# Fifteen small, unread loads on ScalarE's queue between two copies of a decode kernel's prologue

## The chip, the cores and the metric

The kernel runs on one core of a Trainium2 chip. It is compared by device time in microseconds (us): the time from the start to the end of one launch on that core. The core has five engines that run side by side and wait for one another through semaphores: TensorE (PE in the profile, with its weight loads as PEld), VectorE (DVE), ScalarE (ACT), GpSimd (POOL) and SyncE (SP), which computes nothing here and only issues transfers. Transfers run on the core's 16 DMA engines. Both SP and ACT issue transfers in this kernel, each into a queue of its own (in the profile, queue q1 holds those of SP and q10 those of ACT).

## The reference, cut to what matters

One token for each of two sequences goes through attention over a long cache (A) and a small mixer MLP (B), and a gate mixes the two results.

```python
B, Sq, D = 2, 1, 1024
Hq, Hkv, Sk, Dh = 32, 4, 32768, 128
# A: q = x @ wq; scores of 8 query heads per kv head against a cache of 32768 keys
scores = einsum("bhqd,bhkd->bhqk", q, k) * Dh ** -0.5
a = (softmax(scores) @ v) ... @ wo
# B: with one token, the shifted mixing gives zero, so that x1 = x
b = x + gelu(layernorm(x) @ w3) @ w4          # w3: 1024 x 3584
g = sigmoid((x * gate_w).sum(-1))
return g * a + (1 - g) * b
```

All is float32. As the kernel loads them, the two caches, wq, w3, w4 and wo are some 331 MB, nearly all of what is moved.

## The kernel before

**Buffers.** Two large buffers, `ring[0]` and `ring[1]` (`flat` is the same memory seen flat), take turns: each holds one load of up to 128 rows of 64 KB (8 MB; a load of w3 has rows of 56 KB). All large loads are issued by SP, in one fixed order: two of wq, two of w3, then a pair kt and vt (keys and values) for each of the first eight half pairs, two of w4, eight more pairs kt and vt, and three of wo with four small ones into `tail`. `load` (line 222) lets SP wait until the buffer is free and then issues. Each load of `ring[0]` counts up `landed[0]`, each of `ring[1]` counts up `landed[1]`.

**Prologue.** `project` multiplies x by wq as its two parts land (line 361). When both are done, DVE copies half of the product out of PSUM (line 410) and ACT the other half (line 412, `a_q`); q is turned round by small matmuls (line 424) and laid out in `q_pad`. `project` then does the same for the normalised x and w3. Behind that DVE copies one half of the product (line 447, `d_h`) and ACT the other (line 449, `a_h`). DVE waits for both, spreads them (line 454), PE turns them round (28 small matmuls, line 462), and DVE and ACT apply the gelu (lines 466 to 478).

**Loop.** `turn` runs 16 times, once for half of a pair of batch and kv head. PE multiplies the keys (line 495, tile `sc`), DVE takes the maximum in two steps (line 574), ACT the exponentials (line 556), PE transposes them (line 508), and PE multiplies the values (line 517, tile `pv`). Two events of a turn free the buffers. DVE counts up `k_free` ahead of its second maximum (line 573), and SP then issues the next kt into `ring[0]`. The last matmul with the values is marked, and SP then issues the next vt into `ring[1]`. After eight turns `weigh` multiplies by w4, after the other eight by most of wo; a short tail ends the kernel.

**What sets the order.** Every engine runs its list in program order, and a wait holds up all that stands behind it on that engine. PE's list in the prologue is: product with wq, line 424, product with w3, line 462, first turn. DVE's list has lines 447, 454 and 466 to 478 ahead of the loop. ACT's list has line 412, line 449, line 471 and then its loop. SP's third and fourth loads behind wq (the first kt and the first vt) wait only for the two parts of the product with w3; the second kt waits for the `k_free` of the first turn.

## Time and profile before

| | us |
|---|---|
| median of 2 runs | 773.12 (773.07 to 773.16) |
| the profiled execution's own time | 773.08 |
| span of its trace, first to last instruction | 771.5 |
| PE busy (matmuls) | 472.2 (61% of the span) |
| DVE busy | 124.2 (16%) |
| ACT busy | 72.1 (9%) |
| mean granted TensorE clock | 0.772 of full speed |

The profiled execution is 0.04 us below the median, so its rows can stand for the runs. Times in the trace count from the start of the span. In a row of the timeline the first number is the start, the second the duration from the first to the last of the instructions merged into the row; what stands in brackets is how long the engine had been idle and what ended that. A row of the transfers gives the tile, the issuing queue and the time from issue to landing.

### The profile page before, as it was taken

To read this page: it belongs to the slowest core of one execution; us is meant where nothing else is said; L and a number is where in the kernel's file an instruction comes from. 1 tells how busy PE (TensorE), PEld (TensorE's weight loads), DVE (VectorE), ACT (ScalarE), POOL (GpSimd) and SP (SyncE) were. 2 spreads that over 40 slices of the span, in tenths; PEclk is the share of its full clock that TensorE was granted. 3 is DMA by queue.
4 is the path that set the end of the run, shared out by engine and by line. 5 is a ranking of instruction groups with operands and counts; after the bars stand their busy time and mean duration, and the time that the engine had idled before them with its cause. 6 is when DMAs were issued, how large, how long until landed. Compare 5 with 4: busy or idle time off the path is not lost. (4 is left out here: it accounts for less than half of the span.)

```text
span 771.5 us, 7731 instructions
## 1 busy us (share of the span) xinstructions
PE 472.2 (61%) x3316; PEld 243.6 (32%) x3316; DVE 124.2 (16%) x383; ACT 72.1 (9%) x153; POOL 4.4 (1%) x13
## 2 busy tenths in 40 slices
PE   0566765756465756465665364657564657564668
PEld 0233432434232433242331132324342324342323
DVE  1110130212020212120210020202020202020220
ACT  0000020102020102020100020202020202020200
POOL 2000000000000000000000000000000000000000
PEclk9967677677877677877676687777687777687779
DMA  9999999999999999999999999999999999999997
GB/s 381 435 436 436 435 436 436 435 435 432 435 432 435 432 432 435 435 435 435 430 428 443 432 435 435 435 432 435 435 435 435 425 435 435 432 435 425 441 419 329
DMA packets 6646, 331.46 MB, mean 430 GB/s; under 512 B 872, under 2 KB 1008, under 8 KB 1264
## 3 DMA queue, kind: packets, MB, share of 16 engines
q1 hardware_dynamic: 6496, 331.36, 99.4%
q8 instruction: 5, 0.08, 0.0%
q10 hardware_dynamic: 144, 0.01, 0.0%
q14 instruction: 1, 0.01, 0.0%
HBM read 331.36 MB, written 0.01 MB: 429 GB/s over the span
## 5 line engine op out<-in xcount | busy, mean ns | idle before, releaser
L495 PE MATMUL sc<-load,q_cur 128*32 128x512 f32 x1024 | 146.2, 727 | 116.0 <-PEq L53 116.0
L517 PE MATMUL pv<-load,pt 128*32 128x512 f32 x1024 | 125.2, 644 | 18.8 <-PEq L53 18.8
L495 PEld LDWEIGHTS sc<-load,q_cur 128*32 128x32 f32 x1024 | 65.4, 130 | 184.5 <-issue 179.4
L508 PE MATMUL sc<-wide,p 128*128 128x128 f32 x256 | 56.4, 413 | 45.6 <-PEq L53 45.6
L556 ACT ACT_TABLE_LOAD x16 | 20.5, 1283 | 529.3 <-ACTq L53 529.3
L517 PEld LDWEIGHTS pv<-load,pt 128*32 128x32 f32 x1024 | 38.8, 117 | 95.6 <-issue 95.6
L508 PEld LDWEIGHTS sc<-wide,p 128*128 128x128 f32 x256 | 51.9, 225 | 46.6 <-issue 46.6
L574 DVE TENSOR_REDUCE mx<-sc 128x1 f32<-128x512 f32 x32 | 22.1, 692 | 273.6 <-PE sc L495 273.6
L525 PE MATMUL tr<-sel,pv_sb 128*128 128x8 f32 x256 | 37.3, 282 | 23.6 <-PEq L53 23.6
L376 PE MATMUL acc<-load,w_pad 128*32 128x512 f32 x224 | 32.0, 714 | 21.0 <-PEq L53 21.0
L525 PEld LDWEIGHTS tr<-sel,pv_sb 128*128 128x128 f32 x256 | 36.3, 226 | 24.5 <-issue 24.5
L596 DVE COPY pv_sb<-pv 128x512 f32<-128x512 f32 x32 | 20.6, 686 | 137.2 <-PE tr L521 137.2
L591 DVE COPY pt<-sc 64x256 f32<-64x256 f32 x64 | 26.7, 417 | 28.6 <-PE sc L508 28.6
L561 ACT COPY pt<-sc 64x256 f32<-64x256 f32 x64 | 23.5, 368 | 36.2 <-PE sc L508 36.2
L361 PE MATMUL sc<-load,x_pad 128*32 128x512 f32 x128 | 19.6, 779 | 6.5 <-PEq L53 6.5
L376 PEld LDWEIGHTS acc<-load,w_pad 128*32 128x32 f32 x224 | 9.1, 129 | 42.3 <-issue 42.3
L556 ACT ACTIVATE p<-sc,bias 128x512 f32<-128x512 f32 x32 | 21.7, 683 | 0.2
L361 PE MATMUL sc<-load,xn_pad 128*32 128x384 f32 (+1 forms) x128 | 15.6, 648 | 6.2 <-PEq L53 6.2
L499 PE MATMUL tr<-wide,m 128*1 128x128 f32 x16 | 4.3, 269 | 18.8 <-PEq L53 18.8
L588 DVE COPY p<-p 128x256 f32<-128x256 f32 x32 | 9.4, 294 | 38.0 <-ACT p L556 38.0
L346 PE MATMUL tr<-xg_sb,perm 128*128 128x16 f32 x4 | 1.0, 372 | 23.3 <-DMA xg_sb<-xg 23.3
L501 PE MATMUL tr<-ones,mb 1*128 1x1 f32 x32 | 5.9, 253 | 11.4 <-PEq L53 11.4
(101 smaller groups left out, 141.8 us busy)
## 6 DMA issues: line engine op xcount, KB each, us to landing
load<-w SPq DMA_DIRECT2D x4, 7168.0 KB, 25.4
load<-wo SPq DMA_DIRECT2D x1, 7168.0 KB, 27.5
load<-wo SPq DMA_DIRECT2D x1, 4608.0 KB, 18.6
load<-wo SPq DMA_DIRECT2D x1, 2560.0 KB, 24.3
tail<-wo SPq DMA_DIRECT2D x1, 1024.0 KB, 26.3
tail<-wo SPq DMA_DIRECT2D x1, 640.0 KB, 27.4
load<-kt SPq DMA_DIRECT2D x16, 29.3
load<-vt SPq DMA_DIRECT2D x16, 30.9
```

What stands on the lines that cost most here:

```text
L361: last = nc.tensor.matmul(b[C * g:C * g + C, :hi - lo], pad[:, k], t[:, o + lo:o + hi], start=(k == 0), stop=(k == KD - 1))
L376: inst = nc.tensor.matmul(acc[lo:lo + C], lhsT, rows[:, g * (D // 2):(g + 1) * (D // 2)], start=False, stop=last, skip_group_check=True)
L495: last = nc.tensor.matmul(sc[i][C * g:C * g + C], q_cur[:, w, s], ring[0][:, w, o:o + 512], start=(s == 0 and w == 0), stop=(s == 1 and w ...
L508: last = nc.tensor.transpose(sc[k][:, t * P:(t + 1) * P], pair.rearrange("p w q -> p (w q)"), ident)
L517: last = nc.tensor.matmul(pv[C * g:C * g + C], pt[:, w, lo:lo + C], ring[1][:, w, o:o + G * DH], start=(w == 0 and t == 0), stop=(w == PAR ...
L525: last = nc.tensor.matmul(tr[1][:, w * REP:(w + 1) * REP], pv_sb[:, s, w].rearrange("p i q -> p (i q)"), sel[:, s], start=(s == 0), stop=( ...
L556: nc.scalar.activation(p[:, i, :, :PART], sc[i].rearrange("p (t q w) -> p t w q", t=NT, w=PART), AF.Exp, bias=bias, scale=scale, accum_out ...
L561: nc.scalar.copy(*halves(1, c)).then_inc(pt_in, 1)
L574: last = nc.vector.reduce_max(out=mx[:, i:i + 1], in_=sc[i], axis=AX.X)
L588: nc.vector.tensor_copy(p[:, i, :, PART], p[:, i, :, 0]).then_inc(to_pe, 1)
L591: nc.vector.tensor_copy(*halves(0, c)).then_inc(pt_in, 1)
L596: last = nc.vector.tensor_copy(pv_sb[:, :, :, i], pv.rearrange("p (s q w) -> p s w q", q=HALF, w=PART))
```

## The change

Directly behind its copy of wq's product (line 412), ACT waits for that copy and then issues fifteen loads into a new tile `told_sb` of 16 partitions. Load number n, from 1 to 15, has n rows, each of 16 + n floats (68 to 124 bytes), taken from the corner of the first keys. Each adds 16 to a new semaphore `told` when it has landed, and ACT's next instruction waits for all fifteen. Nothing reads `told_sb`. No other instruction, buffer or wait is changed.

```diff
+    told_sb = new("told_sb", 15, 32, parts=16)
...
+    told = sem("told")
...
     act.after(done)
     a_q = act.mark(nc.scalar.copy(row[:, 1], sc[1]))
+    act.after(a_q)
+    for n in range(1, 16):
+        nc.scalar.dma_start(told_sb[:n, n - 1, :16 + n], kt[0, 0, :n, :16 + n]).then_inc(told, 16)
+    act.after((told, 15 * 16))
```

On ACT, in the prologue, the list before reads as follows; L412 is the copy of wq's product, L449 that of w3's product, and L556 is in the loop.

```order
L336 ACT_TABLE_LOAD
L336 ACTIVATE gate<-tr 128x2
L412 COPY pt<-sc 128x512 [waits pe]
L449 COPY pt<-sc 128x384 [waits pe]
L471 ACTIVATE u<-u 128x112 [waits dve]
L553 UNCONDITIONAL_BRANCH
L556 ACT_TABLE_LOAD [waits b_in]
```

The two copies stood next to each other; their line numbers in the changed kernel are 414 and 455. On ACT with the change, the first of the new loads stand like this behind the first copy.

```order
L338 ACT_TABLE_LOAD
L338 ACTIVATE gate<-tr 128x2
L414 COPY pt<-sc 128x512 [waits pe]
L417 DMA told_sb<-kt 1x17 [waits act]
L417 DMA told_sb<-kt 2x18
L417 DMA told_sb<-kt 3x19
```

The first load waits for the copy ahead of it, and the others follow without a wait. The end of the same stretch of ACT's list, up to the gelu (L477), is this.

```order
L417 DMA told_sb<-kt 13x29
L417 DMA told_sb<-kt 14x30
L417 DMA told_sb<-kt 15x31
L455 COPY pt<-sc 128x384 [waits pe,told]
L477 ACTIVATE u<-u 128x112 [waits dve]
L559 UNCONDITIONAL_BRANCH
L562 ACT_TABLE_LOAD [waits b_in]
```

The copy of w3's product now waits for `told` beside PE; no other row of ACT has moved. The lists of PE, DVE, POOL and SP are what they were, but for line numbers.

## The prediction

> **What bounds the kernel now.** I read the page first: the span, the slices of DMA and the queues.

> ```profile
> span 771.5 us, 7731 instructions
> DMA  9999999999999999999999999999999999999997
> q1 hardware_dynamic: 6496, 331.36, 99.4%
> q10 hardware_dynamic: 144, 0.01, 0.0%
> ```

> SP's queue q1 keeps the 16 DMA engines busy for 99.4% of the span. The kernel is bound by its loads. What comes late on an engine costs time only if q1 runs empty by it; then the gap is lost for good, as no slack follows in which to win it back.

> Second I read SP's own waits, to see which events release its loads.

> ```profile
> SPq L222 <- DVEq L573: 323.1, 16, 20.7
> SPq L222 <- PE pv L517: 285.1, 16, 19.5
> ```

> Each kt is released by DVE's line 573, each vt by the values' last matmul. Third I read SP's timeline in the stretch behind the change, and the transfers by window, where a row ends with the time from issue to landing (in this order the two parts of w3, the first kt and vt, the second kt).

> ```profile
> 36.07 16.84 SPq L222 DMA_DIRECT2D load<-w  x2
> ...
> 52.58 0.33 SPq L222 DMA_DIRECT2D load<-w  x1
> 71.26 0.33 SPq L222 DMA_DIRECT2D load<-kt  x1
> 86.26 0.33 SPq L222 DMA_DIRECT2D load<-vt  x1
> 105.38 0.33 SPq L222 DMA_DIRECT2D load<-kt  x1
> 125.25 0.33 SPq L222 DMA_DIRECT2D load<-vt  x1
> ...
> load<-w SPq DMA_DIRECT2D x1, 7168.0 KB, 24.3
> ...
> load<-w SPq DMA_DIRECT2D x1, 7168.0 KB, 24.7
> ...
> load<-kt SPq DMA_DIRECT2D x1, 25.4
> load<-vt SPq DMA_DIRECT2D x1, 29.7
> ...
> load<-kt SPq DMA_DIRECT2D x1, 29.9
> ```

> The first row merges the two issues of w3: the first part is issued at its start, 36.07, and lands at 36.07 + 24.3 = 60.4, the second at 52.58 + 24.7 = 77.3, the first kt at 71.26 + 25.4 = 96.7, the first vt at 86.26 + 29.7 = 116.0, the second kt at 105.38 + 29.9 = 135.3. The spacings are 16.9, 19.4, 19.3 and 19.3: the loads stream without a gap. A load has 8 rows for each engine (128 over 16), so a 64 KB row takes 19.35 / 8 = 2.42 us, a row of w3 2.11 us.

> **How a small load from ACT fares beside that stream.** The trace has one: xg, 128 rows of 96 bytes, issued together with the first load of wq. The rows are from the window of the two issues, and from the window 4 to 23.2 us.

> ```profile
> xg_sb<-xg ACTq DMA_DIRECT2D x1, 12.0 KB, 22.5
> load<-wq SPq DMA_DIRECT2D x1, 22.3
> ...
> q1 hardware_dynamic: 144, 8.39, 100.9%
> q10 hardware_dynamic: 144, 0.01, 0.5%
> ```

> ```profile
> q1 hardware_dynamic: 1, 0.00, 11.2%
> ...
> q10 hardware_dynamic: 1, 0.00, 9.4%
> ...
> q1 hardware_dynamic: 1, 0.07, 2158.9%
> ```

> The semaphore's write of wq's load goes first, then xg's, then the next 64 KB row (0.07 MB). They alternate here too, so I count each such write as a turn.

> [...]

> **How the new loads spread.** What counts is the engine that gets most. No load of fewer than 128 rows stands in the trace, but a store does: the result, 8 rows, seen in the window 770 to 771.5.

> ```profile
> q1 hardware_dynamic: 16, 0.01, 2.1%
> out<-out_sb SPq DMA_DIRECT2D x1, 8.0 KB
> ```

> 16 packets: 8 rows and 8 writes of the semaphore, thus 8 engines with a row each. So load n uses n engines, one row and one write on each. If they always begin at the same engine, that engine serves all fifteen: 30 packets, 30 turns. If they were spread evenly, each engine would have 2 x 120 / 16 = 15. I take 30, since nothing in the row of the store speaks of a rotation; the other is a rival. [...]

> **The cost, step by step.** ACT's part of the prologue, and the issue of four small loads on SP's queue:

> ```profile
> 52.59 0.59 ACT L412 COPY pt<-sc 128x512 f32<-128x512 f32 x1 [24.11 <-PE sc L361]
> 86.27 0.48 ACT L449 COPY pt<-sc 128x384 f32<-128x384 f32 x1 [33.09 <-PE sc L361]
> 740.49 1.86 SPq L222 DMA_DIRECT2D tail<-wo  x4
> ```

> 1. Issuing: 15 x 1.86 / 4 = 7.0 us on ACT, from 53.2 to 60.2. ACT then idles until 86.27, so this costs nothing.
> 2. The turns. The first new packet is there about a microsecond after 53.2. From then to its end the first part of w3 has some 2 rows and its semaphore's write left on each engine, which is 3 turns; the second part gives 9 (8 rows, 1 write), kt 9, vt 9: 30 in all. The thirtieth lies at the end of the first vt, at 116.0 or up to 1.5 us sooner on an engine that runs ahead. It cannot lie much later, either: SP has nothing behind that vt until the second kt is released, and an engine with an empty q1 takes ACT's packets one after the other (0.5% of the engines' time for 144 of them, or 0.5% x 16 x 19.2 / 144 = 0.01 us each). With half a microsecond for the last write to be seen, the wait ends at T = 114.5 to 116.5. I take 115.3.
> 3. What the wait holds up. Line 449 starts at T in place of 86.27. Line 454 on DVE, line 462 on PE and then the first turn stand behind it, while PE has nothing else in its list.

> ```profile
> 87.00 2.08 DVE L454 COPY p<-pt 128x896 f32<-128x896 f32 x2
> 89.13 5.85 PE L462 MATMUL tr<-wide,p 128*128 128x8 f32 x28 [2.92 <-DVE p L454]
> 96.75 8.52 PE L495 MATMUL sc<-load,q_cur 128*32 128x512 f32 x64 [1.77 <-PEq L53]
> 105.44 0.69 DVE L574 TENSOR_REDUCE mx<-sc 128x1 f32<-128x512 f32 x1 [2.85 <-PE sc L495]
> ```

> From the copy to the matmuls of line 462: 89.13 - 86.27 = 2.9; these 5.85; then the keys at once, as the first kt has long landed (before, PE waited 1.77 for it); from their start to the release of the second kt 105.38 - 96.75 = 8.6. Together 17.3: the second kt is issued at T + 17.3 = 132.6, not at 105.38. DVE's gelu (lines 466 to 478) fits beside the keys, as before.
> 4. The gap. A load into an empty queue lands 22.3 after its issue (wq's row), so the second kt lands at 132.6 + 22.3 = 154.9, not at 135.3: 19.6 later. With the ends of T it is 18.8 to 20.8.
> 5. What is late next: the second vt. Before, it was issued 19.9 behind the second kt, and 1.1 of that was the wait for the first vt, which landed at 116.0 while the copies ahead were done at 115.0 (row below). So it is issued 18.8 behind, at 151.4, and could land at 173.7 from an empty queue; in the stream it lands at 154.9 + 19.35 = 174.3. No second gap, by 0.6 us. From there on all waits are as before, 19.6 later.

> ```profile
> 114.57 0.42 DVE L591 COPY pt<-sc 64x256 f32<-64x256 f32 x1 [0.44 <-PE sc L508]
> 116.12 9.07 PE L517 MATMUL pv<-load,pt 128*32 128x512 f32 x64 [1.59 <-PEq L53]
> ```

> 6. The 240 new packets themselves: 0.01 us each, 30 of them on one engine, 0.3 us; inside the ends of T. The one more semaphore and the unread tile cost nothing that a row shows.

> The sum is 19.6 us on the profiled execution's 773.08, which is 792.7; the median of the runs is 773.12, so the same. For the bounds: the nearest rows for 30 turns are xg's 9 turns in 22.5 us. From below, the wait is free as long as the second kt is still issued by 135.3 - 22.3 = 113.0, thus T up to 95.7; this is turn 20. A gain is excluded, since the change takes no byte and no wait away. From above the gap ends with q1 empty.

> **The rivals.**
> - *Spread evenly* (the loads rotate over the engines): 15 turns, 12 by 77.3 and 3 more of 2.42, so T is about 85, ahead of 86.27. Then line 449 doesn't move, and the time is 773.1. It decides from turn 20 downwards. For it speaks that the engines of a short transfer can't be named from the trace; against it nothing does but the plainness of a fixed start. The same 773.1 follows if several packets of one queue go in a turn; xg's row speaks against that.
> - *In between*: some packets pass without a full turn, and the wait ends between turn 21 and 27. Each turn saved takes 2.42 from the loss; at turn 27, T is near 109 and the time 786.
> - *Later than the empty queue*: all rows of a load on one engine. Then it has 120 + 15 packets, 105 of which are left when q1 is empty; at 0.01 us each that is 1 us, at 0.05 each 5 us: 794 to 798. The store's 8 writes speak against it.
> - *The change doesn't do what it says*, because ACT's wait isn't on the way to anything: excluded by step 3, since DVE's line 454 waits for both copies.

> **How the numbers follow.** The forecast 0.77; spread evenly, or several packets in a turn, 0.12; in between 0.07; later 0.04. The forecast's own range is 790.5 to 795.5 (the ends of T, and a microsecond each way for the chain's 17.3). The range of 0.8 takes in most of the forecast, the upper end of the in-between (784 to 788) and the lower of the later: 784 to 797. 2%, about what a measurement of this kernel can tell from no change, is 15.5 us, so the bound lies at 788.6: slower 0.81, within 2% 0.18 (the 0.12 and most of the in-between), faster 0.01.

> **What would show it.** In the profile after: q10 with 144 + 240 = 384 packets; ACT's copy of w3's product at 114.5 to 116.5, ahead of it a wait for `told` and not for PE; the first matmuls with the keys directly behind line 462's; SP's issue of the second kt near 132.6; the slices of DMA with a hole of nearly one slice (19.3 us) near 116 to 135; all later issues of SP 19 to 20 us behind those of before. It is wrong if that copy stays at 86.3 (then the turns are 15 or fewer), if it comes between 96 and 110, or if a second gap opens behind the second kt.

## The result and the profile after

The changed kernel takes 793.54 us (2 runs, 793.35 to 793.72) against 773.12 before: slower by 2.64% (ratio 1.0264, 95% interval 1.022 to 1.0308). The profiled execution's own time is 793.72, its span 792.2 us, 20.7 longer than before.

The page after, its span, its slices of DMA and its two queues:

```profile
span 792.2 us, 7747 instructions
DMA  9999972999999999999999999999999999999997
q1 hardware_dynamic: 6496, 331.36, 96.9%
q10 hardware_dynamic: 384, 0.03, 0.0%
```

SP's queue moves the same packets, but there is a hole in the sixth and seventh slice, and its share falls from 99.4% to 96.9%. ACT's queue has 240 packets more. The timeline of ACT around the hole shows where it begins:

```profile
50.87 0.58 ACT L414 COPY pt<-sc 128x512 f32<-128x512 f32 x1 [22.79 <-PE sc L363]
51.49 5.56 ACTq L417 DMA_DIRECT2D told_sb<-kt  x15
114.66 0.48 ACT L455 COPY pt<-sc 128x384 f32<-128x384 f32 x1 [63.21 <-DMA told_sb<-kt]
```

The fifteen loads are issued in 5.56 us, and the copy of w3's product, at 86.27 before, starts at 114.66. What ends its wait is no longer PE's product, but the small loads. The waits of the stretch 50 to 140 us (engine and line, what it waited for, total, times, longest) show who was held up by it:

```profile
ACT pt L455 <- DMA told_sb<-kt: 63.2, 1, 63.2
...
PE tr L468 <- DVE p L460: 31.0, 1, 31.0
DVE p L460 <- ACT pt L455: 28.1, 1, 28.1
```

DVE waits 28.1 us for ACT's copy, and PE behind it 31.0. The timeline of DVE, PE and SP, taken engine by engine, carries this on to the loads:

```profile
115.24 2.08 DVE L460 COPY p<-pt 128x896 f32<-128x896 f32 x2 [28.11 <-ACT pt L455]
...
117.38 6.14 PE L468 MATMUL tr<-wide,p 128*128 128x8 f32 x28 [31.00 <-DVE p L460]
123.45 8.99 PE L501 MATMUL sc<-load,q_cur 128*32 128x512 f32 x64
...
86.44 0.33 SPq L224 DMA_DIRECT2D load<-vt  x1
132.57 0.33 SPq L224 DMA_DIRECT2D load<-kt  x1
149.31 0.33 SPq L224 DMA_DIRECT2D load<-vt  x1
```

The second kt is issued at 132.57 in place of 105.38. The windows 117 to 132, 132 to 134 and 149 to 150 us of the transfers show the queue empty and then full again:

```profile
DMA packets 1, 0.02 MB, mean 1 GB/s; under 512 B 0, under 2 KB 0, under 8 KB 0
...
q8 instruction: 1, 0.02, 0.4%
...
load<-kt SPq DMA_DIRECT2D x1, 22.9
...
load<-vt SPq DMA_DIRECT2D x1, 25.5
```

In 15 us a single packet moves, a piece of the program (queue q8). The second kt lands at 132.57 + 22.9 = 155.5 (before 135.3, so 20.2 later), the second vt at 149.31 + 25.5 = 174.8, again 19.3 behind it: no second gap opens between the two.

### The profile page after: what moved, and what is told of

The parts are those of the page before. It is cut to its first block, busy times and chain, and to the rows that moved or that the text cites. A ratio compares the mean times of both kernels' runs of the same rounds, so it can differ in the third digit from the quotient of the medians.

```text
span 792.2 us, 7747 instructions
## 1 busy us (share of the span) xinstructions
PE 467.0 (59%) x3316; PEld 236.0 (30%) x3316; DVE 125.2 (16%) x383; ACT 72.0 (9%) x153; POOL 4.2 (1%) x13
## 3 DMA queue, kind: packets, MB, share of 16 engines
q1 hardware_dynamic: 6496, 331.36, 96.9%
## 5 line engine op out<-in xcount | busy, mean ns | idle before, releaser
L501 PE MATMUL sc<-load,q_cur 128*32 128x512 f32 x1024 | 149.2, 741 | 113.2 <-PEq L53 113.2
L523 PE MATMUL pv<-load,pt 128*32 128x512 f32 x1024 | 119.5, 620 | 16.8 <-PEq L53 16.8
L501 PEld LDWEIGHTS sc<-load,q_cur 128*32 128x32 f32 x1024 | 60.6, 133 | 189.4 <-issue 184.9
L562 ACT ACT_TABLE_LOAD x16 | 20.5, 1283 | 521.7 <-ACTq L53 521.7
L602 DVE COPY pv_sb<-pv 128x512 f32<-128x512 f32 x32 | 20.6, 686 | 129.5 <-PE tr L527 129.5
L597 DVE COPY pt<-sc 64x256 f32<-64x256 f32 x64 | 26.7, 417 | 28.4 <-PE sc L514 28.3
L468 PE MATMUL tr<-wide,p 128*128 128x8 f32 x28 | 6.1, 362 | 31.0 <-DVE p L460 31.0
L468 PEld LDWEIGHTS tr<-wide,p 128*128 128x128 f32 x28 | 6.0, 331 | 31.7 <-DVE p L460 31.7
## 6 DMA issues: line engine op xcount, KB each, us to landing
load<-w SPq DMA_DIRECT2D x4, 7168.0 KB, 26.1
load<-wo SPq DMA_DIRECT2D x1, 7168.0 KB, 27.5
load<-wo SPq DMA_DIRECT2D x1, 2560.0 KB, 24.3
```

Of the source, the lines that this page charges most:

```text
L468: last = nc.tensor.matmul(ht_ps[:, o:o + PAIRS], both[:, c, w].rearrange("p i q -> p (i q)"), compact, start=True, stop=True)
L501: last = nc.tensor.matmul(sc[i][C * g:C * g + C], q_cur[:, w, s], ring[0][:, w, o:o + 512], start=(s == 0 and w == 0), stop=(s == 1 and w ...
L523: last = nc.tensor.matmul(pv[C * g:C * g + C], pt[:, w, lo:lo + C], ring[1][:, w, o:o + G * DH], start=(w == 0 and t == 0), stop=(w == PAR ...
L562: nc.scalar.activation(p[:, i, :, :PART], sc[i].rearrange("p (t q w) -> p t w q", t=NT, w=PART), AF.Exp, bias=bias, scale=scale, accum_out ...
L597: nc.vector.tensor_copy(*halves(0, c)).then_inc(pt_in, 1)
L602: last = nc.vector.tensor_copy(pv_sb[:, :, :, i], pv.rearrange("p (s q w) -> p s w q", q=HALF, w=PART))
```

## The experiments

Each kernel is the changed one with one edit. A time is the median of its runs (2 to 10), compared with the kernel before, run on the same chip (773.06 to 773.20 there). The turns are counted by the rule of the prediction. "Copy" is the start of ACT's copy of w3's product and "second kt" the time of its issue; both are from one profiled execution. In ten and twelve that execution was the slowest of the runs: 776.23 and 782.32 us.

| kernel | turns on the busiest engine | copy, us | second kt, us | time, us | ratio to before (95%) |
|---|---|---|---|---|---|
| before | - | 86.27 | 105.38 | 773.12 | 1 |
| the change | 30 | 114.66 | 132.57 | 793.54 | 1.0264 (1.022 to 1.0308) |
| wait_at_end | 30 | 86.15 | 106.92 | 773.29 | 1.0003 (0.9993 to 1.0012) |
| one_row | 30 | 114.61 | 132.44 | 793.69 | 1.0268 (1.0251 to 1.0285) |
| rows120 | 9 | 85.70 | 106.46 | 773.13 | 1.0000 (0.9991 to 1.001) |
| rows127 | 128 | 115.50 | 133.45 | 794.39 | 1.0274 (1.0257 to 1.0291) |
| twelve | 24 | 102.77 | 120.25 | 781.37 | 1.0106 (1.0089 to 1.0123) |
| ten | 20 | 95.14 | 113.97 | 774.79 | 1.0022 (1.0012 to 1.0031) |
| rows16 | 30 (all engines) | 116.50 | 135.10 | 795.74 | 1.0299 (1.0281 to 1.0316) |
| wait_behind_copy | 30 | 85.55 | 116.45 | 778.39 | 1.0065 (1.0049 to 1.0082) |
| on_sp | none | 86.14 | 107.77 | 774.23 | 1.0013 (1.0003 to 1.0022) |

**The wait or the loads: wait_at_end.** The loads stay; ACT waits for them only ahead of its last copy.

```diff
-    act.after((told, 15 * 16))
...
         line.after(ENDED)
+        if line is act:
+            act.after((told, 15 * 16))
```

> The fifteen loads stay where they are; ACT waits for them only ahead of its last copy (the output), not ahead of its copy of w3's product. Theory (the loss is the wait, held until the busiest DMA engine has passed 30 packets in turn with the large loads): ACT's copy is back at 86.3 us, the second kt is issued near 105, the time is 773.1 to 773.6. Rival (the 240 small packets themselves slow the stream of large loads): 785 to 793.5 still.

773.29. The fifteen loads with their 240 packets cost nothing that this can measure (the interval of the ratio ends at 1.0012, 0.9 us), as long as nobody waits for them in the prologue. The loss is the wait. The second kt is issued at 106.92, not near 105; this costs nothing either, as it lands at 106.92 + 28.7 = 135.6, 0.3 behind that of before.

**The busiest engine or the sum: one_row, rows120, rows127, rows16.** In one_row each of the fifteen loads has one row:

```diff
-        nc.scalar.dma_start(told_sb[:n, n - 1, :16 + n], kt[0, 0, :n, :16 + n]).then_inc(told, 16)
+        nc.scalar.dma_start(told_sb[:1, n - 1, :16 + n], kt[0, 0, :1, :16 + n]).then_inc(told, 16)
```

> All fifteen loads have one row each (17 to 31 floats): 15 rows and 15 semaphore writes, not 240 packets. Theory (turns on the busiest engine, and the loads all start at the same engine): still 30 turns there, ACT's copy at 114 to 116 us, 792.5 to 794.5. Rival (the sum of packets or rows counts, an eighth of it here, or loads rotate over the engines, 2 turns each): the wait ends before 86 us and the time is 773.1.

Its queue q10, on the page of one_row, with ACT's wait from its waits between 50 and 125 us:

```profile
q10 hardware_dynamic: 174, 0.01, 0.0%
...
ACT pt L455 <- DMA told_sb<-kt: 63.2, 1, 63.2
```

144 of the 174 packets are xg's, so 30 are left, an eighth of the 240, and ACT waits for exactly as long as with the full change. The sum of packets doesn't set the wait, and the loads don't rotate over the engines: then each engine would have had two.

The same trace shows the turns themselves. The windows 56 to 58.4, 58.4 to 75.4, 75.4 to 94.75 and 94.75 to 114.1 us are, for the engine that serves the small loads, the end of the first part of w3, its second part, the first kt and the first vt. Queue q10 in each:

```profile
q10 hardware_dynamic: 3, 0.00, 0.1%
...
q10 hardware_dynamic: 9, 0.00, 0.0%
...
q10 hardware_dynamic: 9, 0.00, 0.0%
...
q10 hardware_dynamic: 9, 0.00, 0.0%
```

Three, nine, nine and nine: these are the thirty turns as the prediction counted them, one for each large row and one for each write of a semaphore.

In rows120 and rows127 one load of 120 or of 127 rows stands in place of the fifteen. The edit of rows127 (rows120 has 120 in place of 127):

```diff
-    told_sb = new("told_sb", 15, 32, parts=16)
+    told_sb = new("told_sb", 32)
...
-    for n in range(1, 16):
-        nc.scalar.dma_start(told_sb[:n, n - 1, :16 + n], kt[0, 0, :n, :16 + n]).then_inc(told, 16)
-    act.after((told, 15 * 16))
+    nc.scalar.dma_start(told_sb[:127, :31], kt[0, 0, :127, :31]).then_inc(told, 16)
+    act.after((told, 16))
```

> One load of 120 rows (31 floats each) in place of the fifteen: as many rows in all. Theory (turns; 120 rows go to 15 engines, 8 rows and a semaphore write on each): 9 turns, the wait ends near 75 us, ahead of 86.3, and the time is 773.1 to 773.6. Rival (the number of rows sets the wait): 793.5.

> One load of 127 rows (31 floats each) in place of the fifteen. [...] Theory with that rule: some 30 turns until the first vt has ended at 115 us, the other 98 packets one after the other at 0.01 to 0.05 us each, so ACT's copy comes at 116 to 120 us and the time is 794 to 798. It also measures what is left when SP's queue is empty. Rival (rows spread over the engines as evenly as they can, 8 or 9 turns): 773.1.

The page of rows120 and then that of rows127, the queue q10:

```profile
q10 hardware_dynamic: 279, 0.03, 0.0%
```

```profile
q10 hardware_dynamic: 272, 0.03, 0.0%
```

Less xg's 144 these are 135 packets (120 rows, 15 writes of the semaphore, so 15 engines) and 128 (127 rows, one write, so one engine). In the window 52 to 73.5 us of rows120 all 135 pass, well ahead of the copy, which then waits for PE alone. Seven rows more thus cost 21.3 us: 773.13 against 794.39. In rows127 28 of the 128 packets pass between 52 and 114.15 us. The window 114.15 to 115.2 us, behind the last row of the first vt on this engine, shows what it does once SP's queue is empty:

```profile
q10 hardware_dynamic: 100, 0.01, 7.7%
q1 hardware_dynamic: 1, 0.00, 0.1%
```

A hundred packets in one microsecond, 7.7% x 16 x 1.05 / 100 = 0.013 us each. So 98 packets more than in the change moved the copy only from 114.66 to 115.50, half a microsecond ahead of the 116 to 120 that were expected; the time lies within its 794 to 798. The expected time takes all 127 rows to stand on one engine; no run before this one shows that, and here the 128 packets with a single write do, 28 of them beside the large rows and 100 in one microsecond behind them. The 0.05 us a packet at the upper end of the expected cost is not shown here.

In rows16 all fifteen loads have 16 rows:

```diff
-        nc.scalar.dma_start(told_sb[:n, n - 1, :16 + n], kt[0, 0, :n, :16 + n]).then_inc(told, 16)
+        nc.scalar.dma_start(told_sb[:, n - 1, :16 + n], kt[0, 0, :16, :16 + n]).then_inc(told, 16)
```

> All fifteen loads have 16 rows: 240 rows and 240 semaphore writes, twice the packets, 15 rows on each of the 16 engines. Theory (turns of the busiest engine): 30 turns as before, now on every engine, so the latest engine sets the end: ACT's copy at 115 to 117 us, time 793 to 796. Rival (the sum of packets counts): twice the packets, with q1 empty long before they are through, at least 2 us more than with fifteen different sizes, 797 or more.

Twice the packets (q10 has 624, less xg's 144 they are 480, 30 for each of 16 engines) on the same 30 turns; the copy comes at 116.50, 1.84 later, and the time is 795.74 (4 runs, 795.55 to 797.54). That lies within what the theory gave and 1.3 below the rival's bound, which one of the four runs passes. The trace decides between the two. In the window 115.7 to 115.9 us the last packets of both queues stand side by side:

```profile
q10 hardware_dynamic: 3, 0.00, 1.0%
q1 hardware_dynamic: 2, 0.00, 0.6%
```

From 115.9 to 134 us neither queue moves anything. So the small packets do not outlast the first vt by any time, as the rival had it. Every engine now has 30 turns, and the wait ends with the last engine: the copy at 116.50 stands 0.6 behind the end of the window to 115.9.

**How the wait grows with the turns: twelve, ten.** Only the loads of 1 to 12 rows, then of 1 to 10:

```diff
-    for n in range(1, 16):
+    for n in range(1, 13):
...
-    act.after((told, 15 * 16))
+    act.after((told, 12 * 16))
```

> Only the loads of 1 to 12 rows. Theory (24 turns on the busiest engine, the last three of them behind rows of the first vt): ACT's copy near 102.4 us, 12.3 ahead of that with fifteen, and the loss smaller by as much: 20.4 - 12.3 = 8.1, time 780 to 783. Rival (the wait ends with the first vt, however many small packets stand there): 793.5. Rival (a price per load): 20.4 x 12 / 15 = 16.3, time 789.4.

> Only the loads of 1 to 10 rows. Theory (20 turns on the busiest engine; the wait costs nothing as long as it ends by about 95): the twentieth turn lies at the end of the first kt, ACT's copy comes at 94.5 to 96.5 us, 8 to 10 later than without loads, and the time is still 773.1 to 775. The two points with twelve loads (copy at 102.77, loss 8.2) and fifteen (114.66, 20.4) drawn out as a line reach zero at 94.7. Rival (a price per load, from the run with twelve: 8.2 / 12 each): 780.

ACT's copy in the timeline of twelve, then of ten:

```profile
102.77 0.48 ACT L455 COPY pt<-sc 128x384 f32<-128x384 f32 x1 [50.85 <-DMA told_sb<-kt]
```

```profile
95.14 0.48 ACT L455 COPY pt<-sc 128x384 f32<-128x384 f32 x1 [43.91 <-DMA told_sb<-kt]
```

From 20 to 24 turns the copy moves by 7.63, from 24 to 30 by 11.89: 1.9 and 2.0 us a turn, a little under a row's 2.42, because one turn in each step is against a semaphore's write, which costs next to nothing: in the profile after, SP's queue passes 16 small packets from 113 to 116 us in 0.3% of the engines' time, 0.3% x 16 x 3 / 16 = 0.01 us each. The times follow: 774.79, 781.37, 793.54. The losses of the executions whose copies these are, against the medians of before, are 3.0, 9.2 and 20.6 (776.23, 782.32, 793.72). So with ten loads the copy comes 8.9 us later than before and most of that is free. What is lost, 1.6 us by the median and 3.0 in the profiled execution, is more than the 0.4 that the expected line gives; that line set copies of profiled executions against median losses. In twelve a second gap shows too: its second vt lands at 139.71 + 24.3 = 164.0, 20.5 behind its second kt (120.25 + 23.3 = 143.55), where a load takes 19.3. The cause of that was not traced.

**Which work the wait holds up: wait_behind_copy.** The loads stay; ACT waits behind its copy of w3's product, ahead of the gelu.

```diff
-    act.after((told, 15 * 16))
...
     a_h = act.mark(nc.scalar.copy(row[:, 1, :F // G - 512], sc[3][:, :F // G - 512]))
+    act.after((told, 15 * 16))
```

> The loads stay, and ACT waits for them behind its copy of w3's product, ahead of the gelu. Theory (the wait ends at 114.7 as before, and what counts is the chain from there to the release of the second kt): PE's small matmuls and the first keys are no longer held, only the gelu's end (1.5 us) and DVE's two maxima, so the second kt is issued near 117, not 132.6, lands near 140, 4.7 later than without loads, and the time is 777 to 779.5. Rival (the loss is the time for which ACT stands still, 28 us of which 20 show): 793.5.

ACT, PE and SP in its timeline:

```profile
85.55 0.48 ACT L454 COPY pt<-sc 128x384 f32<-128x384 f32 x1 [33.19 <-PE sc L363]
115.05 0.30 ACT L477 ACTIVATE u<-u 128x112 f32<-128x112 f32 x1 [29.02 <-DMA told_sb<-kt]
...
88.41 6.14 PE L468 MATMUL tr<-wide,p 128*128 128x8 f32 x28 [2.92 <-DVE p L460]
96.94 9.45 PE L501 MATMUL sc<-load,q_cur 128*32 128x512 f32 x64 [2.39 <-PEq L53]
...
116.45 0.33 SPq L224 DMA_DIRECT2D load<-kt  x1
```

ACT waits for the same loads to the same time, and the loss is 5.3 us (778.39 against 773.13) in place of 20.4. From the wait's end to the issue of the second kt it is now 116.45 - 115.05 = 1.4, not 17.9: PE's small matmuls and the first keys are done while ACT waits. So it isn't the length of ACT's wait that is paid, but where in the chain to `k_free` it ends.

**The queue: on_sp.** SP issues the fifteen loads behind its second load of w3; ACT's wait is unchanged.

```diff
     load(flat[1][:, :PART * 2 * F], run(w3, 1), landed[1], at("q1"))
+    sp.after((act.sem, 3))
+    for n in range(1, 16):
+        nc.sync.dma_start(told_sb[:n, n - 1, :16 + n], kt[0, 0, :n, :16 + n]).then_inc(told, 16)
...
-    act.after(a_q)
-    for n in range(1, 16):
-        nc.scalar.dma_start(told_sb[:n, n - 1, :16 + n], kt[0, 0, :n, :16 + n]).then_inc(told, 16)
```

> SP issues the same fifteen loads, behind its second load of w3 and after ACT's copy of wq's product; ACT's wait stays where it is. Theory (small packets wait only for turns against another queue; in q1 itself they stand behind w3's rows and pass at some 0.01 us each): the wait ends near 78 us, ahead of 86.3, and the time is 773.1 to 774. Rival (a small load has a fixed price, whatever its queue): 785 to 793.5.

The timeline of ACT and SP in on_sp:

```profile
86.14 0.48 ACT L455 COPY pt<-sc 128x384 f32<-128x384 f32 x1 [33.27 <-PE sc L366]
...
52.90 5.26 SPq L262 DMA_DIRECT2D told_sb<-kt  x15
```

The same loads, issued behind the same copy and waited for at the same place, are through before 86.14 when they stand in SP's queue: ACT again waits for PE. What costs 20 us from ACT's queue costs 1.1 us from SP's (774.23 against 773.13, with 774 at most expected; the interval of the ratio, 1.0003 to 1.0022, is 0.2 to 1.7 us).

## Why the prediction was right, point by point

The forecast of 792.7 was off by 0.84 us. Three terms were off by some 0.6 us each, T downwards, the chain and the landing upwards. T and the chain cancel (the second kt was forecast for 132.6 and issued at 132.57); that is luck.

- *Issuing costs nothing.* 5.56 us measured (7.0 forecast), beside an idle ACT. wait_at_end shows that issue and packets together are free.
- *Turns.* Thirty on the busiest engine: shown by one_row (30 packets in all, the same wait, and 3, 9, 9 and 9 of them beside the four loads), rows120 (9 turns, no wait) and on_sp (no turns, no wait). T was forecast at 115.3 and is 114.66, 0.6 behind the last small packet at 114.06: the busiest engine is one that runs ahead. In the trace of the change 7 of the 16 semaphore writes of the first vt come between 114.1 and 115.5 us, behind the last small packet. The step's second half, that the wait can't end much later than the first vt, is shown by rows127 for 98 packets more.
- *All begin at the same engine.* This was chosen against an even spread, and no row of before could decide it. one_row excludes the even spread; which engine it is no run names.
- *The chain from T to the second kt.* 17.3 forecast, 132.57 - 114.66 = 17.9 measured: to line 462's matmuls 2.7 (2.9 forecast), these 6.1 (5.85), the keys to the release 9.1 (8.6). PE's two stretches were a little slower than the rows of before. That the loss hangs on this chain was shown by wait_behind_copy, where only 1.4 us stand behind the same wait and the loss falls to 5.3.
- *The gap.* A load into the empty queue took 22.9, not 22.3; 20.2 measured against 19.6. The span grew by 20.7; the missing 0.5 comes in at one load. The second part of w4 still lands 20.1 later than before (414.91 + 26.0 against 394.60 + 26.2), the first kt behind w4 20.7 later (432.18 + 28.6 against 411.67 + 28.4). PE's product with w4 releases that kt; why it came later there stays open.
- *No second gap.* Right, but not by the margin forecast: the second vt was issued 16.7 behind the second kt, 2 us sooner than forecast, and landed 19.3 behind it. The 2 us are the matmuls with the values, which the forecast took over from before. They took 7.07 us in place of 9.07, at a granted clock of 1.00 in place of 0.77. Their row in the profile after, then the windows 142 to 149.3 us after and 116 to 125.2 us before (the clock stands ahead of the last two numbers):

```profile
142.19 7.07 PE L523 MATMUL pv<-load,pt 128*32 128x512 f32 x64 [0.75 <-PEq L53]
...
142.00:149.30 7.30, 7.11 (x65) 2.50 (x65) 0.22 (x1) 0.00 (x0) 0.00 (x0) 1.00 1.00 433
...
116.00:125.20 9.20, 9.08 (x65) 2.60 (x65) 0.00 (x0) 0.00 (x0) 0.00 (x0) 0.77 1.06 458
```

- *The free part of the wait.* Forecast to reach to T = 95.7, some 20 turns. With ten loads T was 95.14, and the execution with this T lost 3.0 us (1.6 by the median), so this bound was too high: the chain's 17.3 and the landing's 22.3 from which it was worked out were both too short. In that execution the chain took 113.97 - 95.14 = 18.8 and the landing 24.2, so that the wait would have been free up to 135.3 - 24.2 - 18.8 = 92.3. T passed this by 2.8, about what was lost. Most of the longer chain is the keys: 10.0 us from their start to the release, at a granted clock of 0.71, where 8.6 was forecast from a row at 0.82.

Of the rivals, the even spread and the passing of several packets in a turn fell with one_row and with the change's own 114.66: ACT waited 63.2 us for the thirty in one_row, and 3, 9, 9 and 9 of them passed beside the four loads. Against several in a turn speaks rows127 too, where all 128 packets belong to a single load and 28 of them had passed by 114.15 us. The case later than the empty queue was made in rows127, and came to 0.85 us, with 0.013 us a packet, not the 0.05 of this rival's upper end.

## What to carry to other kernels

In this kernel a small transfer beside a saturated queue paid for its packets on the busiest engine: each waited for one packet of the other queue, 2.42 us for a 64 KB row, and the write of the semaphore was a packet too. So count packets on the busiest engine, not bytes or transfers; one load of 120 rows was free where fifteen with the same rows cost 20 us, and so were those fifteen when their landing was awaited later. What a late engine costs is read from where the loads' queue would run empty. Up to there a delay is free: with ten loads some 6 of 8.9 us. Behind it a delay is paid nearly in full: from twelve loads to fifteen 11.9 us of it cost 11.4 in the profiled executions and 12.2 by the medians.

## What the runs showed that was not expected

on_sp lost 1.1 us where 0.9 at most was forecast. In the window 76.3 to 78.7 us, on_sp and then the kernel before:

```profile
DMA packets 34, 0.66 MB, mean 274 GB/s; under 512 B 24, under 2 KB 24, under 8 KB 24
```

```profile
DMA packets 18, 1.05 MB, mean 437 GB/s; under 512 B 2, under 2 KB 2, under 8 KB 2
```

Of the 24 small packets in on_sp two are writes of w3's load, as in the window of before; 22 are of the new loads, where most of the 240 had passed by 76.3 (232 small packets in the window 74 to 76.3 us, w3's writes among them). Of the large rows, 34 - 24 = 10 stand in this window in place of 18 - 2 = 16. The lag was not made up in the stream behind it: in the profiled execution of on_sp (774.68) the first kt lands at 70.96 + 27.4 = 98.4, the first vt at 117.7 and the second kt at 137.0, each 1.7 later than before, and the output is issued at 771.83, 1.6 later than the 770.19 of before. Why these few packets took so much longer than the 0.013 us of rows127 stays open.
